# Loading and transposing all four token blocks ahead of the first w1 piece in a dense SiLU layer

## The chip, the cores and the metric

The kernel runs on one core of a Trainium2 chip. The metric is device time in microseconds of one execution. The kernel before was run five times: 128.04, 128.56, 125.96, 125.98 and 127.38 us, with a median of 127.38 us. The first of these executions, 128.04 us, is the one that was profiled; the span of its instructions is 126.7 us.

## The reference

The layer multiplies 2048 tokens of width 640 by a 640 x 1728 matrix, applies SiLU, and multiplies by a 1728 x 640 matrix. Everything is bfloat16.

```python
def reference(x, w1, w2):                      # x [1, 2048, 640], w1 [640, 1728], w2 [1728, 640]
    h = jnp.einsum("bsd,df->bsf", x, w1)
    h = jax.nn.silu(h)
    return jnp.einsum("bsf,fd->bsd", h, w2)
```

## The kernel before, in words

TensorE contracts over the 128 partitions, so the first product needs x transposed, with the width 640 on the partitions. The tile `xT` holds it as five slices of 128 (`DT` = 5) by 2048 tokens. The hidden activations `hT` are produced transposed as well: 13 tiles of 128 hidden columns (`FT` = 13) and a tail of 64 (`FL`). Tokens are worked in four chunks of 512 (`SCH`). One tile of one chunk is five matmuls of 128 x 128 weights against 512 tokens, accumulated in one PSUM bank; ScalarE then applies SiLU into `hT`.

The first chunk is special, because the kernel wants to begin before much has arrived. Its four blocks of 128 tokens, x0 to x3 in this text, are loaded plainly into the tile `x0` (one slice per block) and transposed on TensorE by the helper `turn` (lines 175 to 199). One `turn` waits for its block and for its two PSUM banks, issues five 128 x 128 transposes (line 182), and then has VectorE copy three of the five slices (line 185) and ScalarE copy the other two (line 193) into `xT`. `turn` returns the points in time of these two copies. Blocks 0 and 2 use banks 7 and 6, blocks 1 and 3 use banks 5 and 4, so the turn of block 2 waits for the copies of block 0, and the turn of block 3 for those of block 1. The chunks 1 to 3 come through transposing DMA loads (line 158) straight into `xT`.

The first three hidden tiles (`FA` = 3) of the first chunk are called the opening here. Their columns of w1 are loaded in three pieces along the contraction: piece 0 is slice 0 (96 KB), piece 1 is slices 1 and 2 (192 KB), piece 2 is slices 3 and 4 (192 KB); see `ks` in line 127 and `load_ks` in line 129. The remaining columns of w1 follow in three larger loads (`FG`, line 120).

All these loads are issued from two queues. SP issues, in this order: x0, x1, piece 1, x2, x3, the three larger w1 loads, the fifteen transposing loads, and the w2 loads. ScalarE's queue issues piece 0 and piece 2.[...] The code of each engine is a straight list, executed in order: an engine that waits for a semaphore holds back everything that comes behind it in its own list, the DMA issues included.

TensorE's list in the opening is: nine dummy matmuls on a tile of zeros (line 173), the turns of blocks 0 and 1, and then `k_pass` (lines 216 to 228). A `k_pass(k0, k1, j0, j1)` runs the slices k0 to k1 for the three tiles on the token blocks j0 to j1. The order is: piece 0 on block 0, piece 0 on block 1, piece 1 on blocks 0 and 1, the turn of block 2, piece 2 on blocks 0 and 1, the turn of block 3, then all five slices on block 2, and all five on block 3 (lines 230 to 243). The last pass releases the three SiLU instructions. After the opening, the loop in line 253 runs the other ten tiles of the first chunk, and the loop in line 260 the other chunks. The second product follows the same way and isn't touched.

## Time and profile before

| Quantity | Value |
|---|---|
| Median of five runs | 127.38 us |
| Lowest and highest run | 125.96 and 128.56 us |
| Profiled execution: its own time, its span | 128.04 us, 126.7 us |
| TensorE matmul busy | 122.2 us, 96% of the span |
| TensorE weight loads busy | 58.5 us, 46% |
| ScalarE busy | 40.5 us, 32% |
| VectorE busy | 9.0 us, 7% |
| Transposes of the opening (line 182) | 20, 2.5 us busy |
| Dummy matmuls (line 173) | 9, 2.1 us busy |
| Read from and written to HBM | 5.16 MB and 2.62 MB |

In the views below, PE is TensorE's matmuls, PEld its weight loads, DVE is VectorE, ACT is ScalarE; a q behind an engine's name means its instruction queue, as in SPq for a DMA issued by SP. L208 is line 208 of the kernel before. `ps` is the PSUM tile, `w1s` the tile that holds w1. Times within an execution are microseconds from the start of the span. Matmuls are pipelined and the ends shown are modelled, so the pace of matmuls is read from how many of them fit in a stretch and not from the length of one.

### The profile page before, as it was taken

Reading aid. Unit: us, or ns where it says so; the run is one execution under the profiler, and the core shown is the slowest. Engines: PE = TensorE matmul, PEld = TensorE weight load, DVE = VectorE, ACT = ScalarE, POOL = GpSimd, SP = SyncE. Lnnn points to the kernel's source line nnn. Section 1 sums busy time; section 2 is a strip of 40 time slices with the busy share of each in tenths; the row PEclk is TensorE's granted clock in tenths of the full one; section 3 lists DMA queues with packets and bytes.
Section 4 is the critical chain, followed back from the end, with each engine's and each line's share of the span. In section 5 each row is a group of like instructions: output and inputs, shape, how many; then the busy total and the mean of one; then the engine's idle time right before and its main releaser. Section 6 shows DMA issues by size and latency. Waiting matters only on the chain.

```text
span 126.7 us, 1446 instructions
## 1 busy us (share of the span) xinstructions
PE 122.2 (96%) x625; PEld 58.5 (46%) x636; DVE 9.0 (7%) x16; ACT 40.5 (32%) x70; POOL 0.8 (1%) x7
## 2 busy tenths in 40 slices
PE   8599999999999999999999999999999999999993
PEld 5386444444444444444444444444444443444452
DVE  0120000000000000000000120200004201012021
ACT  5126555555555555555550101010003011010100
POOL 2000000000000000000000000000000000000000
PEclk9999999999999999999999999999999999999999
DMA  5999944448910000000000000000001575111112
GB/s 153 306 376 227 83 97 96 111 94 280 390 49 0 0 0 3 0 0 0 0 5 0 0 0 0 0 0 0 5 0 41 115 265 210 52 52 57 52 54 101
DMA packets 17878, 10.37 MB, mean 82 GB/s; under 512 B 10832, under 2 KB 17872, under 8 KB 17872
## 3 DMA queue, kind: packets, MB, share of 16 engines
q1 hardware_dynamic: 17456, 9.98, 28.9%
q10 hardware_dynamic: 416, 0.30, 0.8%
q8 instruction: 5, 0.08, 0.3%
q14 instruction: 1, 0.01, 0.0%
HBM read 5.16 MB, written 2.62 MB: 61 GB/s over the span
## 4 chain that ended last, share of the span: by engine, by line
PE 93%; DMA 4%; issue 1%; SPq 1%; ACT 0%
PE ps L208 93%; DMA w1s<-in_w_dram 4%; PE ps L182 1%; SPq L89 1%; ACT o_sb L288 0%; SPq L401 0%
## 5 line engine op out<-in xcount | busy, mean ns | idle before, releaser
L208 PE MATMUL ps<-xT,w1s 128*128 128x512 bf16 (+3 forms) x308 | 60.0, 361 | 1.8 <-DMA w1s<-in_w_dram 1.4
L208 PE MATMUL ps<-w2s,hT 128*128 128x512 bf16 (+2 forms) x216 | 45.0, 366 | 0.4 <-issue 0.2
L208 PEld LDWEIGHTS ps<-xT,w1s 128*128 128x128 bf16 (+1 forms) x313 | 28.6, 101 | 32.3 <-DVE xT L185 1.7
L212 ACT ACTIVATE hT<-ps 128x512 bf16<-128x512 f32 x52 | 30.8, 597 | 23.9 <-PE ps L208 23.9
L208 PEld LDWEIGHTS ps<-w2s,hT 128*128 128x128 bf16 x221 | 20.9, 98 | 24.4 <-issue 1.1
L288 ACT CAST o_sb<-ps 128x512 bf16<-128x512 f32 (+1 forms) x8 | 4.4, 546 | 42.2 <-PE ps L208 42.2
L286 DVE CAST o_sb<-ps 128x512 bf16<-128x512 f32 (+1 forms) x9 | 6.1, 677 | 94.2 <-PE ps L208 91.9
L208 PE MATMUL ps<-hT,w2s 128*128 128x512 bf16 x51 | 11.3, 379 | 0.1
L208 PEld LDWEIGHTS ps<-hT,w2s 128*128 128x128 bf16 x52 | 5.1, 98 | 6.1
L288 ACT CAST oT<-ps 128x512 bf16<-128x512 f32 x2 | 1.1, 589 | 11.0 <-PE ps L208 11.0
L193 ACT COPY xT<-ps 128x256 bf16<-128x256 bf16 x4 | 1.5, 372 | 5.2 <-PE ps L182 5.2
L182 PE MATMUL ps<-ident,x 128*128 128x128 bf16 x20 | 2.5, 288 | 0.0
L173 PE MATMUL ps<-z 128*128 128x256 bf16 x9 | 2.1, 418 | 0.4 <-DVE z L124 0.4
L286 DVE CAST oT<-ps 128x512 bf16<-128x512 f32 x2 | 1.3, 687 | 13.7 <-PE ps L208 13.7
L208 PE MATMUL ps<-w2t,hTt 64*128 64x512 bf16 (+2 forms) x17 | 2.2, 366 | 0.0
L182 PEld LDWEIGHTS ps<-ident,x 128*128 128x128 bf16 x20 | 1.9, 130 | 0.6 <-DMA x<-in_x_dram 0.5
L185 DVE COPY xT<-ps 128x384 bf16<-128x384 bf16 x4 | 1.4, 358 | 7.6 <-PE ps L182 7.6
L151 ACT ACT_TABLE_LOAD x1 | 1.3, 1283 | 1.2 <-PEq L401 1.2
L173 PEld LDWEIGHTS ps<-z 128*128 128x128 bf16 x9 | 1.2, 141 | 0.8 <-DVE z L124 0.4
L212 ACT ACTIVATE hTt<-ps 128x512 bf16<-128x512 f32 x2 | 1.2, 597 | 1.1 <-PE ps L208 1.1
L208 PEld LDWEIGHTS ps<-w2t,hTt 64*128 64x128 bf16 x17 | 0.7, 94 | 1.4 <-issue 0.8
L208 PE MATMUL ps<-hTt,w2t 64*128 64x512 bf16 x4 | 0.6, 382 | 0.0
(10 smaller groups left out, 1.5 us busy)
## 6 DMA issues: line engine op xcount, KB each, us to landing
out_dram<-o_sb SPq DMA_DIRECT2D x15, 160.0 KB, 1.9
w2s<-in_w_dram SPq DMA_DIRECT2D x1, 1120.0 KB, 6.5
w2s<-in_w_dram SPq DMA_DIRECT2D x1, 960.0 KB, 8.9
x<-in_x_dram SPq DMA_DIRECT2D x4, 160.0 KB, 3.5
w1s<-in_w_dram SPq DMA_DIRECT2D x1, 640.0 KB, 6.9
w1s<-in_w_dram SPq DMA_DIRECT2D x1, 560.0 KB, 7.8
w1s<-in_w_dram SPq DMA_DIRECT2D x1, 480.0 KB, 5.7
xT<-in_x_dram SPq DMA_TRANSPOSE x15, 2.8
```

What stands on the lines that cost most here:

```text
L89: return tick(eng.dma_start(out=out_ap, in_=in_ap), s, 16)
L151: act.activation(out=warm[:, :], in_=warm[:, :], func=ACT.Silu)
L173: pe.matmul(ps[:, 3, 0:HB], lhsT=z[:, 0:P], rhs=z[:, :], start=True, stop=True)
L182: ins = pe.transpose(dst, x0[:, j, dt * P:(dt + 1) * P], ident[:, :])
L185: r = tick(dve.tensor_copy(out=xT[:, 0:nv, j * P:(j + 1) * P], in_=v[:, 0:nv * P].rearrange("p (k s) -> p k s", s=P),), s_dve)
L193: r = tick(act.copy(out=xT[:, nv:DT, j * P:(j + 1) * P], in_=a[:, 0:(DT - nv) * P].rearrange("p (k s) -> p k s", s=P),), s_act)
L208: return pe.matmul(o, lhsT=l, rhs=r, start=start, stop=stop, skip_group_check=shared)
L212: r = tick(act.activation(out=out_ap, in_=in_ap, func=ACT.Silu), s_act)
L286: r = tick(dve.tensor_copy(out=out_ap, in_=in_ap), s_dve)
L288: r = tick(act.copy(out=out_ap, in_=in_ap), s_act)
```

## The change

It touches two things. The loads of x2 and x3 are issued ahead of all pieces of w1; piece 0 moves from ScalarE's queue to SP's, behind the four blocks of x and ahead of piece 1; piece 2 stays on ScalarE's queue and moves in its list behind the copy of block 0. And all four turns stand ahead of the first w1 matmul in TensorE's list; `k_pass` takes token columns in place of block numbers, piece 0 is run on the tokens 0 to 255 and then on 256 to 511, and pieces 1 and 2 are run on all 512 tokens at once.

```diff
-        ld_k = [load_ks(act, 0), load_ks(sp, 1)]
         for j in (2, 3):
             ld_x[j] = load(sp, x0[:, j, :], x_v[:, j, :])
+        ld_k = [load_ks(sp, 0), load_ks(sp, 1)]
...
         act.activation(out=warm[:, :], in_=warm[:, :], func=ACT.Silu)
-        ld_k.append(load_ks(act, 2))
...
-        t0 = turn(0, 7, 6)
-        t1 = turn(1, 5, 4)
+        turned = turn(0, 7, 6)
+        ld_k.append(load_ks(act, 2))
+        turned += turn(1, 5, 4) + turn(2, 7, 6) + turn(3, 5, 4)
...
-        def k_pass(k0, k1, j0, j1, last=False):
+        def k_pass(k0, k1, t0_, t1_):
             for ft in range(FA):
-                if k0 == 0 and j0 == 0:
-                    wait(pe, bank_free[ft])
                 for k in range(k0, k1):
-                    ins = mm(
-                        ps[:, ft, j0 * P:j1 * P],
-                        w1s[:, k, ft * P:(ft + 1) * P],
-                        xT[:, k, j0 * P:j1 * P],
-                        start=(k == 0 and j0 == 0), stop=(k == DT - 1), shared=True,
-                    )
-                if last:
+                    ins = mm(ps[:, ft, t0_:t1_], w1s[:, k, ft * P:(ft + 1) * P], xT[:, k, t0_:t1_],
+                             start=(k == 0 and t0_ == 0), stop=(k == DT - 1), shared=True)
+                if k1 == DT:
                     silu(hT[:, ft, 0:SCH], ps[:, ft, :], ft, tick(ins, s_pe))
...
-        wait(pe, *t0, ld_k[0])
-        k_pass(0, 1, 0, 1)
-        wait(pe, *t1)
-        k_pass(0, 1, 1, 2)
-        wait(pe, ld_k[1])
-        k_pass(*ks[1], 0, 2)
-        t2 = turn(2, 7, 6)
-        wait(pe, ld_k[2])
-        k_pass(*ks[2], 0, 2)
-        t3 = turn(3, 5, 4)
-        wait(pe, *t2)
-        k_pass(0, DT, 2, 3)
-        wait(pe, *t3)
-        k_pass(0, DT, 3, 4, last=True)
+        wait(pe, *turned[0:4], ld_k[0])
+        k_pass(0, 1, 0, HB)
+        wait(pe, *turned)
+        k_pass(0, 1, HB, SCH)
+        for i, (a, b) in enumerate(ks[1:]):
+            wait(pe, ld_k[i + 1])
+            k_pass(a, b, 0, SCH)
```

The banks that `bank_free[ft]` in the removed wait names had not been used before, so that wait was empty.

## The prediction

> **What bounds the kernel now.** I read the page's chain of waits first, then its groups, then the chain, the timeline and the transfers of the opening alone.

> ```profile
> PE 93%; DMA 4%; issue 1%; SPq 1%; ACT 0%
> ...
> L208 PE MATMUL ps<-xT,w1s 128*128 128x512 bf16 (+3 forms) x308 | 60.0, 361 | 1.8 <-DMA w1s<-in_w_dram 1.4
> ```

> TensorE carries 93% of the chain, and its w1 matmuls idle 1.8 us before them in all. Only the 4% of DMA and the opening's matmuls are open to the change. The chain in order of time gives the opening:

> ```profile
> 1.03 4.86 DMA w1s<-in_w_dram
> 5.90 0.05 issue
> 5.94 1.46 PE ps L208 x6
> 7.41 0.53 PE ps L182 x5
> 7.94 0.77 PE ps L208 x6
> 8.71 0.28 PE ps L182 x5
> 8.98 1.68 PE ps L208 x30
> 10.66 0.05 issue
> 10.71 10.74 PE ps L208 x49
> ```

> Columns: start, length, what. The 30 narrow matmuls ending at 10.66 finish the three opening tiles; from there TensorE runs without a gap worth naming: 10.74/49 = 0.219 us per full matmul. So **the change is worth what it moves the 10.66.** The lines also show the clock. Five transposes take 0.53 us at 7.41 and 0.28 at 8.71; six 256-column matmuls take 1.46 at 5.94, 0.77 at 7.94. The array doubles its pace near 8.1: with 0.213 us slow and 0.109 fast per 256 columns, 0.77 is one slow and five fast. Before that, per the timeline:

> ```profile
> 2.29 1.34 PE L182 MATMUL ps<-ident,x 128*128 128x128 bf16 x10
> ...
> 3.67 0.37 ACT L193 COPY xT<-ps 128x256 bf16<-128x256 bf16 x1 [0.25 <-PE ps L182]
> ...
> 5.07 0.69 PE L208 MATMUL ps<-xT,w1s 128*128 128x128 bf16 x5 [1.43 <-DMA w1s<-in_w_dram]
> ```

> TensorE turns blocks 0 and 1, then stands 1.43 us until piece 0 of w1. The transfers issued from 1 to 5 us, with their time to landing, and the core's state by microsecond (clock share, DMA share and GB/s last):

> ```profile
> x<-in_x_dram SPq DMA_DIRECT2D x2, 160.0 KB, 4.9
> ...
> w1s<-in_w_dram SPq DMA_DIRECT2D x1, 192.0 KB, 4.9
> w1s<-in_w_dram ACTq DMA_DIRECT2D x1, 192.0 KB, 4.8
> w1s<-in_w_dram ACTq DMA_DIRECT2D x1, 96.0 KB, 4.1
> ```
> ```profile
> 1.00:2.00 1.00, 1.00 (x6) 0.75 (x5) 0.00 (x0) 0.78 (x1) 0.35 (x2) 1.00 0.86 210
> 2.00:3.00 1.00, 1.00 (x9) 0.55 (x8) 0.00 (x0) 0.74 (x2) 0.00 (x0) 1.00 0.90 239
> 3.00:4.00 1.00, 0.64 (x6) 0.37 (x5) 0.68 (x2) 0.70 (x2) 0.00 (x0) 1.00 0.84 257
> 4.00:5.00 1.00, 0.00 (x0) 0.00 (x0) 0.03 (x1) 0.05 (x1) 0.00 (x0) 1.00 0.99 335
> ```

> With the issue times of the timeline (x2 1.50, x3 2.01, pieces 0.80, 1.03, 1.29) they land: piece 0 at 4.9, piece 1 at 5.9, piece 2 at 6.1, x2 at 6.4, x3 at 6.8. The DMA engines are full, so order decides, not issue. The clock column shows 1.00 throughout, so it isn't the one that doubles.

> [...]

> **The change part by part.**

> Matmul shape: 48 matmuls become 18, six of 256 columns and twelve of 512; the columns stay 7,680. The 30 narrow ones ran at 1.68/30 = 56 ns, which is 128 columns at the fast rate with weight loads hidden.[...] Full width by itself is worth nothing.

> Order of transfers. SP now issues x2 at about 1.03, x3 at 1.50, piece 0 at 2.0, piece 1 at 2.45, the next w1 groups some 0.45 us later each (one more issue of 0.43 ahead). Landings I estimate from bytes: by the rates above the core has moved 0.21, 0.45, 0.71 and 1.04 MB by 2, 3, 4 and 5 us. In SP's order x2 is complete at 0.49 MB, x3 at 0.655, piece 0 at 0.75, piece 1 at 0.95: moved by 3.2, 3.8, 4.1 and 4.7. Landing follows by 0.4 us (x0: 0.164 MB moved by 1.8, landed 2.2) up to 1.55 (piece 1 now: 0.82 MB with ACT's two by 4.35, landed 5.9). That gives x3 4.2 to 5.35, piece 0 4.5 to 5.7, piece 1 5.1 to 6.3. With sequential x ahead and no second queue beside it I take the lower part: **x3 4.5, piece 0 5.0, piece 1 5.6.**

> Piece 2 is issued behind ACT's wait for block 0's transposes: at 3.1 to 3.5 instead of 1.29. Time to landing 2.2 (x0, nothing beside it) to 4.8 (itself now): 5.3 to 8.3; I take 7.5. Queued behind the waits on ACT are only the copies and this issue; TensorE waits for it.

> TensorE. Block 2 is turned near 3.7 to 4.2, its banks being free (copies end 4.04). Block 3: 4.5 to 5.03; copies, by the rows 0.37, end by 5.5. The piece-0 matmuls start at **5.05**, as now, but without ten transposes among them later (0.53 + 0.28 us). Six of 256 columns at half rate, at the measured 1.46 with dispatch or 1.28 without: done by 6.4. The new wait for all eight copies stands between the two halves, at 5.7, with the whole opening queued behind it; the copies of block 3 end at 5.5, so I cost it at nothing, and at most the 0.65 us by which block 3 may be later. The removed bank wait was empty. Full matmuls cost 0.427 slow (four times 0.106). By 8.1 four of twelve are done; the other eight take 8 × 0.219 = 1.75: end **9.85** instead of 10.66. Piece 2 is needed at 8.5, one microsecond after I expect it; if it comes at 8.3 it still costs nothing. The next w1 group landed at 2.49 + 5.7 = 8.2, now 8.65: hidden behind the opening. The transposing loads start 0.45 later; their fifth landed at 11.81 + 3.6 = 15.4 and is needed 10.8 us after the opening: covered by five microseconds.

> Sum: −0.8, and I keep −0.7 for hand-over between waits. Own time of the profiled execution: 128.04, its span 126.7 and 1.34 around it; that becomes 127.3. It stands 0.66 above the median 127.38, which becomes **126.7**.

> **The rivals.**

> Early clock. The window 1.3 to 4.7 was busy 1.0 us with dummies and 1.34 with transposes, 69%, and didn't release the clock; 4.7 to 8.1, some 82% busy, did. With two more turns, 1.06 us, in it, the first becomes up to 90%, if transposes count. Then pieces 0 and 1 end at 7.0, piece 2 (7.5) is waited for, end 7.5 + 1.31 = 8.8: −1.85, so 125.5.[...]

> Transfers cancel. With landings at their late ends TensorE, which is in order, stands behind block 3 and starts at 6.1: 2.0/0.427 = 4.7 of 15 by 8.1, the rest 2.26, end 10.36: 127.1. At a start of 6.7 nothing is left of the gain. For it: x3 landed at 6.8 before; against: 0.3 MB of w1 was ahead of it then.

> Slower. If the start slips beyond about 6.2, the window 4.7 to 8.1 holds 1.9 us of matmuls and 0.53 of transposes, 71%, like the one that didn't release the clock; release waits until 11.5. From 6.2 that is 5.3/0.427 = 12.4 matmuls slow, 0.57 for the rest, end 12.05: +1.4, so 128.8; from 7.3, 12.65: +2.0, 129.4. Start later than 6.2 is the point that decides.

> The change doesn't do what it says: partly so, since piece 0 stays in halves of 256; no price.

> **How the numbers follow.** Likeliest case 0.46 (126.1 to 127.2); early clock 0.22 (125.0 to 126.0); cancelled 0.18 (126.8 to 127.7); slower 0.14 (128.2 to 129.6). 2%, about what a measurement of this kernel can tell from no change, is 2.55 us: below 124.83 or above 129.93. No case's centre reaches it. The runs shown spread by 2.6 us, so some chance of each: faster 0.05 from the early clock's edge, slower 0.09 from the late clock with a late piece 2; same 0.86. The range 125.4 to 128.9 leaves out the lowest early-clock times (0.07) and the upper half of the slower case (0.08).

> **What would show it.** Right: ten transposes before the first w1 matmul, that matmul at 4.8 to 5.5 released by piece 0, no wait for piece 2, first 512-column tile after the opening near 9.9, the rest of the span as long as now. Wrong: a start after 6.2, 512-column matmuls at 0.427 us beyond 8.1, a wait for piece 2, or TensorE gaps after the opening.

## The result, and the profile after

Over 41 runs the changed kernel has a median of 127.86 us (126.42 to 128.31); the kernel before, over 78 runs, 128.04 us (125.96 to 129.37). The ratio of the medians is 0.9986 (0.9967 to 1.0008, from resampling the runs), that of the means 1.0000 (0.9982 to 1.0018): no change that can be told. A ratio of each kernel's fastest runs alone, those within 1.5% of its own fastest, reads 1.0062 (1.0039 to 1.0084), but that leaves out 43 of the 78 runs of before and none of after, so everything below uses all runs.

The equal medians hide two different shapes. Before falls into two groups: 16 of 78 runs lie under 127.0 us, none between 127.0 and 127.25, and the others reach up to 129.4. After has 3 of 41 under 127.0, and nothing above 128.31. **The change took away the best runs and the worst ones.**

The page of after, chain by engine and the costliest group:

```profile
PE 93%; DMA 3%; SPq 1%; issue 1%; ACT 0%
...
L208 PE MATMUL ps<-xT,w1s 128*128 128x512 bf16 (+2 forms) x278 | 59.9, 384 | 0.6 <-DMA w1s<-in_w_dram 0.4
```

The idle time ahead of the w1 matmuls fell from 1.8 to 0.6 us, and yet the span is 126.8 us where it was 126.7. The chain in order of time (start, length, what):

```profile
1.97 3.72 DMA w1s<-in_w_dram
...
5.73 5.49 PE ps L208 x20
11.22 0.05 issue
11.27 10.74 PE ps L208 x49
```

TensorE begins on w1 at 5.73, when piece 0 lands, 0.66 us later than before. The 20 matmuls are the 18 of the opening and two of the next tile; two full ones are 0.44 us, so the opening ends at 10.78, against 10.66. How fast it ran is seen at its weight loads, one for each matmul of 512 columns (start, length, engine, line, operation, shapes; the last line holds five):

```profile
7.42 0.15 PEld L208 LDWEIGHTS ps<-xT,w1s 128*128 128x128 bf16 x1 [0.27 <-issue]
7.84 0.15 PEld L208 LDWEIGHTS ps<-xT,w1s 128*128 128x128 bf16 x1 [0.28 <-issue]
8.27 0.15 PEld L208 LDWEIGHTS ps<-xT,w1s 128*128 128x128 bf16 x1 [0.28 <-issue]
8.70 0.15 PEld L208 LDWEIGHTS ps<-xT,w1s 128*128 128x128 bf16 x1 [0.27 <-issue]
9.11 0.96 PEld L208 LDWEIGHTS ps<-xT,w1s 128*128 128x128 bf16 x5 [0.27 <-issue]
```

Up to 9.1 us they follow each other by some 0.43 us, which is half rate, and from there by 0.22. So the doubling came at 9.1; before it was at 8.1. And the transfers of after issued from 2.9 to 3.3 us and from 1.4 to 2.1 us (pieces 2 and 0, and among the rest the blocks of x):

```profile
w1s<-in_w_dram ACTq DMA_DIRECT2D x1, 192.0 KB, 4.7
```
```profile
x<-in_x_dram SPq DMA_DIRECT2D x2, 160.0 KB, 2.8
w1s<-in_w_dram SPq DMA_DIRECT2D x1, 96.0 KB, 3.7
```

The blocks come quickly (2.8 us, where x2 took 4.9 before); piece 0 lands at 5.69, piece 2, issued at 3.09, at 7.8.

One relation holds through all profiled executions and says where to look. A kernel's own time less the end of its opening is 128.04 − 10.66 = 117.38 before, 128.25 − 10.78 = 117.47 after, and between 117.38 and 117.48 in the fourteen more taken below. (In e2, e7 and e11 the record of one opening matmul is missing, and the end is counted with it.) Nothing after the opening moves, in any of them. A run of 126.3 us, of which no profile was taken, should by this have had an opening that ended near 8.9.

### The profile page after: what moved, and what is told of

Read it like the earlier page. It is cut to its first block, busy times and chain, and to the rows that moved or that the text cites. A ratio compares the mean times of both kernels' runs of the same rounds, so it can differ in the third digit from the quotient of the medians.

```text
span 126.8 us, 1386 instructions
## 1 busy us (share of the span) xinstructions
PE 123.1 (97%) x595; PEld 57.2 (45%) x606; DVE 9.0 (7%) x16; ACT 40.5 (32%) x70; POOL 0.8 (1%) x7
## 4 chain that ended last, share of the span: by engine, by line
PE 93%; DMA 3%; SPq 1%; issue 1%; ACT 0%
PE ps L208 93%; DMA w1s<-in_w_dram 3%; SPq L89 1%; ACT o_sb L275 0%; SPq L388 0%
## 5 line engine op out<-in xcount | busy, mean ns | idle before, releaser
L208 PE MATMUL ps<-xT,w1s 128*128 128x512 bf16 (+2 forms) x278 | 59.9, 384 | 0.6 <-DMA w1s<-in_w_dram 0.4
L208 PE MATMUL ps<-w2s,hT 128*128 128x512 bf16 (+2 forms) x216 | 45.0, 366 | 0.4 <-issue 0.2
L208 PEld LDWEIGHTS ps<-xT,w1s 128*128 128x128 bf16 (+1 forms) x283 | 27.3, 101 | 33.1 <-issue 1.4
L208 PEld LDWEIGHTS ps<-w2s,hT 128*128 128x128 bf16 x221 | 20.9, 98 | 24.4 <-issue 1.1
L208 PE MATMUL ps<-hT,w2s 128*128 128x512 bf16 x51 | 11.3, 379 | 0.1
L208 PEld LDWEIGHTS ps<-hT,w2s 128*128 128x128 bf16 x52 | 5.1, 98 | 6.1
L208 PE MATMUL ps<-w2t,hTt 64*128 64x512 bf16 (+2 forms) x17 | 2.2, 366 | 0.0
L208 PEld LDWEIGHTS ps<-w2t,hTt 64*128 64x128 bf16 x17 | 0.7, 94 | 1.4 <-issue 0.8
L208 PE MATMUL ps<-hTt,w2t 64*128 64x512 bf16 x4 | 0.6, 381 | 0.0
```

The source lines that it names most:

```text
L208: return pe.matmul(o, lhsT=l, rhs=r, start=start, stop=stop, skip_group_check=shared)
```

## The experiments

My theory after the result: **which run is fast is decided by the moment at which the array's clock doubles**, which is drawn anew in each run, and the change shifts the odds. The rival: only the landings of the transfers and TensorE's start matter. Each kernel ran beside the kernel before; in its several sessions that had medians of 127.70 to 127.99 us, and 54 of 206 runs under 127.0.

| Run | What it is | Runs | Median, us (lowest to highest) | Under 127.0 | Ratio of medians to before |
|---|---|---|---|---|---|
| e1 | before, 6 dummies behind block 1 | 22 | 126.80 (125.76 to 129.19) | 13 | 0.991 (0.990 to 0.998) |
| e9 | before, 3 dummies behind block 0, 4 behind block 1 | 22 | 126.42 (125.97 to 127.11) | 20 | 0.990 (0.988 to 0.998) |
| e3 | before, 1 dummy in place of 9 | 20 | 128.42 (127.38 to 129.33) | 0 | 1.004 (1.001 to 1.007) |
| e4 | after, 1 dummy in place of 9 | 22 | 128.12 (126.96 to 129.50) | 1 | 1.002 (0.999 to 1.004) |
| e2 | after, 6 dummies in the gaps | 14 | 127.40 (126.80 to 128.00) | 3 | 0.996 (0.992 to 1.001) |
| e7 | e2 with piece 2 early | 18 | 126.88 (126.48 to 128.99) | 11 | 0.993 (0.991 to 0.997) |
| e11 | e2 with pieces 0 and 2 early | 22 | 127.25 (126.78 to 129.45) | 5 | 0.997 (0.995 to 1.003) |
| e5 | the new order of loads alone | 6 | 130.62 (128.61 to 131.49) | 0 | 1.022 (1.006 to 1.029) |
| e6 | the new list of TensorE alone | 6 | 129.12 (128.97 to 129.27) | 0 | 1.010 (1.008 to 1.015) |
| e8 | after, opening matmuls 128 wide | 22 | 127.69 (126.13 to 130.00) | 5 | 0.999 (0.996 to 1.004) |
| e10 | after, piece 0 early | 6 | 128.40 (127.98 to 129.37) | 0 | 1.005 (1.002 to 1.014) |
| e12 | after, piece 2 early | 22 | 128.28 (126.67 to 129.09) | 5 | 1.002 (0.995 to 1.006) |
| e13 | before again | 18 | 127.95 (126.19 to 129.12) | 6 | 1.000 (0.991 to 1.002) |
| e14 | after again | 18 | 127.82 (126.29 to 128.64) | 2 | 0.999 (0.996 to 1.001) |

### More and fewer dummies in the kernel before (e1, e9, e3)

```diff
         t0 = turn(0, 7, 6)
+        dummies(3)                  # e9 alone
         t1 = turn(1, 5, 4)
+        dummies(6)                  # e1: 6, e9: 4
```

e3 has `dummies(1)` in place of `dummies(9)`.

> The kernel before with six more dummy matmuls behind the turn of block 1, in the 1.43 us in which TensorE stood. Theory clock phase (the runs of before fall in two groups, 16 of 78 under 127.0 us[...]): with TensorE busy from 0.4 us on, nearly every run falls in the low group, median 126.0 to 126.8, all runs within 1.5 us. Rival transfers (only the landing of the w1 pieces and TensorE's start, 5.07 before and 5.73 after, decide): nothing changes, median 128.0 with the same two groups.

> The kernel before with three dummy matmuls behind the turn of block 0 and four behind that of block 1 (the first filled kernel had six behind block 1 and its profile still stood 1.05 us for block 1, and it had 13 of 22 runs under 127.0 us). Clock phase: the burst from 0.4 to 5 us has no hole, so over 75% of the runs are under 127.0 us, median 126.1 to 126.7. Rival: the rest of the high runs come from late transfers and not from the clock, the share stays near 60% and the median at 126.8.

> The kernel before with one dummy matmul in place of nine. Clock phase: the first burst is cut by 1.7 us, so the low group goes: no run under 127.0, median 128.2 to 128.7. Transfers: 128.0, low group as before.

Dummies compute nothing and touch no transfer, and they decide: the share of runs under 127.0 goes from 0 of 20 with one dummy to 54 of 206 with nine, in the runs beside the experiments, and 20 of 22 with sixteen and no hole. The rival said that e1 changes nothing and that e9 does no better than e1. (In a chain, a step that follows another on TensorE begins at that one's modelled end, about 0.2 us behind its first matmul; real starts are taken from timelines.) In e3's chain the pace stays at half rate to the end of the opening's turns:

```profile
7.11 0.53 PE ps L182 x5
7.65 1.28 PE ps L208 x6
8.93 0.53 PE ps L182 x5
9.46 2.14 PE ps L208 x30
```

The transposes at 8.93 still take 0.53 us, and the end is 11.60. The chain of e9 is one of TensorE alone; a line of its timeline, below it, has the real start of the w1 matmuls:

```profile
4.21 0.85 PE ps L173 x4
5.06 1.46 PE ps L210 x12
6.52 0.28 PE ps L182 x5
6.80 0.65 PE ps L210 x6
7.46 0.28 PE ps L182 x5
7.74 1.68 PE ps L210 x30
```
```profile
4.85 1.67 PE L210 MATMUL ps<-xT,w1s 128*128 128x128 bf16 x12
```

The same order of work and of loads as before, starting at 4.85, against 5.07; both turns take 0.28 us, the end is 9.41, and the 4.86 us of DMA have gone from the chain. e9 has the lowest median of this study, ahead of both kernels compared here. e1 missed part of its runs, probably because block 1 can be late: in its one profile (128.12 us) TensorE stood for it, 1.05 us by the pace of the transposes, which is the hole that e9's three dummies shorten, and the doubling came at 7.8.

### The same kernels once more (e13, e14)

> The kernel before, unchanged, for one more profile. Clock phase: if its time is under 127.0 us, the first w1 matmuls run at full rate (128 columns in 0.056 us from 5 us on) and the opening ends near 9.0; if it is above 127.5, they run at half rate and the opening ends at 10.4 or later. Transfers: the opening's end follows the landing of pieces 1, 2 and block 3, whatever the pace of the matmuls.

> The changed kernel, unchanged, for one more profile. Clock phase: start of the w1 matmuls 5.4 to 6.1 us again, end of the opening between 9.2 (clock early, then held by piece 2) and 11.2 (clock at 10), by the pace of the matmuls. Transfers: the end is again 10.6 to 10.8.

The profile of e13, time 128.38, is a slow draw of the kernel before. Its chain:

```profile
7.14 0.53 PE ps L182 x5
7.67 1.28 PE ps L208 x6
8.95 0.35 PE ps L182 x5
```

The six matmuls that took 0.77 us in the first profile take 1.28, all at half rate; the doubling falls into the transposes at 8.95. With 30 narrow matmuls in 1.68 us from 9.30, the opening ends at 10.98, 0.3 us later, and the time is 0.34 us longer. The transfers don't explain it: piece 1, on which the six matmuls from 5.68 waited, landed at 5.63, against 5.89 in the first profile. The profile of e14 is an early draw of the changed kernel (TensorE, start, length, and what ended the idle time before):

```profile
3.95 0.45 PE L181 MATMUL ps<-ident,x 128*128 128x128 bf16 x5 [0.34 <-DMA x<-in_x_dram]
4.57 0.45 PE L181 MATMUL ps<-ident,x 128*128 128x128 bf16 x5 [0.16 <-DMA x<-in_x_dram]
5.08 2.49 PE L208 MATMUL ps<-xT,w1s 128*128 128x256 bf16 x12
9.17 1.04 PE L208 MATMUL ps<-xT,w1s 128*128 128x512 bf16 x4 [1.60 <-DMA w1s<-in_w_dram]
```

The turns are already fast, the w1 matmuls begin at 5.08, as I had forecast, and pieces 0 and 1 are through by about 7.5. Then TensorE stands 1.60 us for piece 2. Its chain names it: the DMA issued at 3.11 took 6.01 us.

```profile
3.11 6.01 DMA w1s<-in_w_dram
```

Time 128.02: **in this run the early clock was given back, almost all of it, to the wait for piece 2.** Without it the opening would have ended near 9.0. The start, 5.08, is earlier than the 5.4 to 6.1 of the clock theory's expectation, and the end, 10.64, lies in both of them, so it doesn't part them; the pace does.

### Fewer and more dummies in the kernel after, and piece 2 (e4, e2, e7, e12)

```diff
         turned = turn(0, 7, 6)
-        ld_k.append(load_ks(act, 2))       # e7, e12: moved up, behind the first SiLU
-        turned += turn(1, 5, 4) + turn(2, 7, 6) + turn(3, 5, 4)
+        dummies(2)                         # e2, e7; e12 without dummies
+        turned += turn(1, 5, 4)
+        dummies(1)
+        turned += turn(2, 7, 6)
+        dummies(1)
+        turned += turn(3, 5, 4)
+        dummies(2)
```

> The kernel after with one dummy matmul in place of nine. Clock phase: the few low runs (3 of 41) go, the rest stays, since its window is filled by turns and matmuls from 3.4 us on: median 127.8 to 128.2. If transposes don't count as busy, this kernel is as late as the kernel before with one dummy. Transfers: 127.9.

> The kernel after with six more dummy matmuls spread over the gaps between its four turns and the first w1 matmul. Clock phase: TensorE is busy throughout, the clock doubles by about 7 us at the latest, median 126.4 to 127.0, 0.2 to 0.6 us above the filled kernel before, because piece 2 lands at 7.8 us. Transfers: 127.9, as after.

> The filled kernel after (median 127.40) with piece 2 issued on ACT's queue at once, as before the change, in place of behind block 0's copy. Theory late piece 2 (with the clock early, TensorE stood in that kernel until piece 2 landed at 8.92 us): the wait goes, the opening ends near 8.6 instead of 9.6, median 126.5 to 126.9. Rival shared bandwidth (192 KB of piece 2 delay x2, x3 and piece 0 by as much as they save): 127.2 to 127.6, with TensorE's start moved from 5.1 to 5.8 or later.

> The changed kernel with piece 2 issued on ACT's queue at once, nothing filled. Clock phase: most runs have the clock late, and then piece 2 (landed at 7.8) is not waited for, so the bulk stays at 127.3 to 128.3; only the early-clock runs gain: low group larger than 3 of 41, lowest run near 126.0, median 127.4 to 127.8. Rival (piece 2 is what costs in the bulk too): the whole distribution shifts down by 0.4 us or more, median below 127.4.

Filling helps the changed kernel less than half as much as the other: 127.40, above my 127.0. The chain of e2 has the reason, piece 2 again, landed at 8.92:

```profile
3.07 5.85 DMA w1s<-in_w_dram
8.92 0.05 issue
8.97 0.61 PE ps L214 x2
```

With piece 2 issued at once (e7) the median falls to 126.88, as the theory of the late piece said. Its profile (127.08 us) bears out a part of the rival too: the w1 matmuls start at 6.03 where e2 started them at 5.12, because a block of x came late, and the opening ends at 9.70 and not at the forecast 8.6. But the cost of that lies in e12, the same move without dummies: 5 of 22 runs are under 127.0, yet the bulk moved up, to 129.09, which neither theory had. In e12's chain x2 took 3.73 us, and the last two blocks are turned together at 4.80 where after turned them at about 3.9 and 4.7:

```profile
1.03 3.73 DMA x<-in_x_dram
4.75 0.05 issue
4.80 1.25 PE ps L182 x10
6.05 0.64 PE ps L208 x3
```

Here blocks 2 and 3 were late with piece 2 beside them, and the first w1 matmul starts at 5.84 (timeline), only 0.11 us behind that of after. The larger part of the 0.6 us by which this opening ends later (11.40) is the clock: full-width matmuls start 0.427 us apart until near 10.1, one microsecond longer than in after, which is worth half of that. Whether the hole ahead of 4.80 caused the late doubling in most runs of e12, one profile can't show. So the four blocks and piece 2 probably compete for the same 4 us (x2 took 3.73 us here, x2 and x3 a median of 2.8 in after). e4 came out where its clock theory had it, 128.12, with too few low runs in either kernel (1 of 22, 3 of 41) to compare. Whether transposes count for the clock as other matmuls do, it doesn't decide; e8's profile does, below.

### One half of the change alone (e5, e6)

e5 takes the changed kernel's loads and the list of TensorE of before; e6 the reverse.

> The new order of loads with TensorE's list as before. Clock phase: TensorE has only two turns and a hole from about 3.7 to 5.7 us, when piece 0 lands, so the low group shrinks or goes, and the start is 0.65 us later than before: median 128.2 to 128.7. Transfers alone: the same start as the changed kernel, blocks 2 and 3 are there when they are needed, median 127.9.

> TensorE's list of the changed kernel with the loads as before. Both theories: TensorE, in order, stands until block 3 (6.8 us) and begins the w1 matmuls at 7.3, 2.2 us later. Clock phase: the hole from 3.7 to 6.4 keeps the clock at half rate until 8 to 11 us in most runs, median 129.2 to 130.2, widest spread of all. Transfers alone: 2.2 us later with the same clock, less the ten transposes, median 129.4.

Either half alone is slower than both together. e5 is worse than either theory had it: its own profile, with the doubling at about 9.0, ends the opening at 11.23 and gives 128.61; three of its six runs are above 130.9. Its TensorE has only two turns to do until piece 0 lands (1.47 us idle in the profile, start 5.57), so I take the slow runs to be ones in which the doubling came later still; no profile of such a run was taken. e6 waits for blocks 2 and 3 and starts at 6.48, where 7.3 was expected; at 129.12 it lies just under the clock theory's 129.2 to 130.2 and 0.3 us under the rival's 129.4, so the median doesn't part them, and in its six runs the spread is the smallest of all and not the widest. So, as these few runs go, the new list of TensorE is needed to fill the hole which the new order of loads makes, and the new order of loads to feed that list in time.

### Width, and piece 0 (e8, e10, e11)

e8 cuts every opening matmul into pieces of 128 columns. e10 issues piece 0 on ScalarE's queue at 0.8 us; e11 does so in e7.

```diff
-        ld_k = [load_ks(sp, 0), load_ks(sp, 1)]     # behind x2 and x3
+        ld_k = [load_ks(act, 0)]                    # e10, e11: ahead of them
...
+        ld_k.append(load_ks(sp, 1))                 # behind x2 and x3
```

> The changed kernel with each opening matmul cut into 128-column ones, 60 in place of 18, the columns the same. My sum[...]: +0.1 us, median 127.9 to 128.1, the same spread. Rival (full width is worth something, by weight loads or dispatch): at half rate or full rate the opening grows by over 0.5 us, median 128.4 or more.

> The changed kernel with piece 0 back on ACT's queue, issued at 0.8 us. Theory late start (TensorE began at 5.73 and not at the forecast 5.05, because piece 0 waits behind four blocks of x on SP's queue): the start goes to 5.0 to 5.3 and the median falls by 0.2 to 0.3 us, since 0.5 us at half rate are worth half of that: 127.5 to 127.7. Rival (the block of x that is held up by piece 0 now sets the start, or the draw of the clock hides it): 127.8 to 128.1.

> The filled kernel after with pieces 0 and 2 both on ACT's queue at once; only the x-first order on SP and the four turns ahead are left of the change. Clock phase with the pieces in time: median 126.4 to 126.8, like the filled kernel before, so that the order of x in itself brings nothing. Rival (all turns ahead makes TensorE wait for block 3 with full queues): 127.0 or more.

Full width is worth nothing that can be seen (the 0.1 us forecast for e8 was an estimate): 60 matmuls give 127.69, 18 gave 127.86, and the interval of the ratio, 0.996 to 1.004, ends short of the rival's 128.4 (1.005). That the spread grew, to 126.13 to 130.00, I had not expected. e10 shows no gain from an earlier piece 0: in its profile block 3 came late and TensorE stood 1.21 us for it, the rival's mechanism at a higher price than it had (128.40). e11, 127.25, points the same way beside e7's 126.88: with x, piece 0 and piece 2 all early it is x3 that is late, and the chain of its profile goes through a block of x and not through w1. Its expected equality with e1 failed. e10's profile holds more. By microsecond (TensorE's busy time second, its clock share third from the end):

```profile
4.00:5.00 1.00, 0.45 (x5) 0.28 (x5) 0.63 (x2) 0.64 (x2) 0.00 (x0) 1.00 0.84 225
5.00:6.00 1.00, 0.17 (x3) 0.17 (x4) 0.02 (x1) 0.03 (x1) 0.00 (x0) 1.00 0.94 275
6.00:7.00 1.00, 0.68 (x9) 0.41 (x7) 0.36 (x1) 0.37 (x1) 0.00 (x0) 1.00 0.88 268
7.00:8.00 1.00, 1.00 (x5) 0.56 (x5) 0.00 (x0) 0.00 (x0) 0.00 (x0) 0.50 0.98 306
...
9.00:10.00 1.00, 1.00 (x3) 0.15 (x1) 0.00 (x0) 0.00 (x0) 0.00 (x0) 0.50 1.09 376
10.00:11.00 1.00, 0.74 (x4) 0.25 (x4) 0.00 (x0) 0.00 (x0) 0.00 (x0) 0.79 1.87 302
```

Here the view records the clock: the array was fast, fell back to half at 7.0 after three microseconds in which TensorE worked 0.45, 0.17 and 0.68 of the time, and returned 0.42 into the eleventh (0.42 at half and 0.58 at full rate make 0.79). From fall to return are 3.4 us. In the same execution piece 2 took 7.35 us.

The array had doubled its pace at 3.6: there the starts of its transposes go from 0.107 to 0.056 us apart. So the pace changed at 3.6, 7.0 and 10.4, with 3.4 us from each to the next. No other profile has a fall on record (the mean granted clock was 0.987 in e10 and 1.0 in the others), so the 3.4 us are those of e10; the other profiles are laid against the same length. A busy share here is the columns at the pace of the moment and not the modelled lengths. In the 14 profiles that show the moment of the first doubling (in e11 and e14 it falls into a gap), the 3.4 us ahead of it were busy for 75% (e7) to 100%, and the 3.4 us ahead of those for at most 70% (e3), in the first profile 61%, in that of after 60%. The transposes are counted in these shares. In e8 the pace doubles at 5.6:

```profile
2.35 2.52 PE L181 MATMUL ps<-ident,x 128*128 128x128 bf16 x20
4.68 2.76 PE L208 MATMUL ps<-xT,w1s 128*128 128x128 bf16 x36
```

The 3.4 us up to there hold 2.0 us of transposes and 0.8 of other matmuls. In e3 1.9 us of other matmuls and 0.5 of transposes, from 3.5 to 6.9, brought no doubling: the transposes at 8.93 still took 0.53. So transposes count here: without them e8's stretch, which the doubling followed, would hold less than e3's. A cause of the two groups is my estimate from these numbers and is not shown: a stretch of 3.4 us that ends before the hole has grown too large brings the doubling, and one that ends later leaves it to the next or the one after. With e10's 3.4 us laid at every position over the profiled openings, all taken as equally likely, and with the 70 to 75% between the shares above as what a stretch needs, the estimate is that the clock doubles ahead of 6 us in 0.2 to 0.45 of the positions before (two profiles), in 0.4 to 0.7 of those of after (two profiles), and in 0.9 of those of e9 and of e2. The low groups are 54 of 206, 5 of 59, 20 of 22 and 3 of 14: by this estimate an early clock mostly doesn't make a low run in the two kernels that issue piece 2 late. For e3 and e4 the estimate gives none (0 of 20 and 1 of 22). For e1 it gives at most 0.3, by a profile in which block 1 was late, where 13 of 22 runs were low; there it falls short.

## Why the prediction was wrong

The time lies inside the range, 0.18 us under the median of before where I forecast 0.7, and the means are equal: a gain isn't there. The base was off as well: the median of before, 127.38 in five runs, is 128.04 in 78, so 126.7 was 0.66 us too low before any step of the argument.

- **"The clock doubles near 8.1", taken for both kernels: the step that failed.** I read one draw out of one profile and used it as a property of the kernel; I then carried a difference of two such sums over to a median. The five times shown (two at 126.0, three from 127.4) already carried the two groups. In the profiled executions the doubling came at 8.1 and about 9.0 before (e13), at 9.1 and before 4 us after (e14). In the profile after, the 3.4 us from 2.3 to 5.7 were busy for 60% and brought no doubling, and 9.1 for 8.1 costs half of 1.0 us, 0.5.
- **Start at 5.05: mis-sized in the profile.** It was 5.73, because piece 0 landed at 5.69, the very end of my 4.5 to 5.7; I had taken 5.0. At half rate 0.68 us are worth 0.34. Together 9.85 + 0.34 + 0.5 = 10.7, against the 10.78 measured: so the saving of the ten transposes fits as forecast, and the two delays ate it. In e14 the same start was 5.08, so this is a draw too.
- **Piece 2 costed at nothing: the second step that failed, by the size of its landing.** I took 7.5, bound 8.3, and covered it by matmuls at half rate that need it at 8.5. It landed at 7.8, 8.92 (e2) and 9.12 (e14), and with the early clock there is little cover. In that rival I had counted a wait of 0.5 us (7.0 to 7.5); it was 1.60. So the early clock, priced at 125.5, gave 128.02 in e14.
- Two readings of the first profile. The clock column, which I set aside because it reads 1.00 throughout, is that of the array: in e10 it follows the fall to half (0.50 from 7.0 on) and the return at 10.4, and misses only the half rate from the start to 3.6. And the 69% for 1.3 to 4.7 us counted the modelled lengths of transposes; by their pace it is some 61%.
- Matmul shape worth nothing (e8), hidden w1 groups, and transposing loads with room to spare: right. No TensorE gap after the opening was found, and own time less opening is the same to 0.1 us.
- The slower rival: not shown in the changed kernel, whose runs end at 128.64. Its 11.5, which is 8.1 and 3.4 us, was an estimate; changes of pace 3.4 us apart are recorded in e10 alone. A doubling that comes late for want of work is what e3 shows in the kernel before, with transposes still at half rate at 8.93 to 9.46 and the end at 11.60, and probably e5.

What the change does is then this. Its turns keep TensorE busier from 3.4 us on (0.98 of the microsecond from 4 to 5 in the profile after, 0.00 in that of before), which probably is why the late draws of before (129 and more) go; the nine dummies are needed too, since e4, with the same turns and one dummy, has 129.27 and 129.50 among its 22 runs. No transposes are left among the matmuls. But an early clock, which in the kernel before should end the opening near 8.9, runs into piece 2 (1.60 us in e14, 0.72 in e8). The means say that gain and loss are equal; the sizes of the parts were not measured. How much of the lost low group is the wait for piece 2 and how much fewer early draws isn't measured either. The estimate from stretches of 3.4 us speaks for the wait, since it has early draws more often in after than before. e12 has more low runs, 5 of 22 against 5 of 59 for after in both series, but moves x as well.

## What to carry to other kernels

Where times spread in two groups, look for a state that is drawn per run, and forecast the odds of each group and not a shift of the median; a single profile is one draw. Keep TensorE busy without a hole from its first microsecond until the real work flows: seven more dummy matmuls in the kernel before, placed where it would have stood, brought 1% in the median (0.7% in the mean) and a spread of 1.1 us, against 2.5 in the runs beside them. And when a change may let an engine run faster, cost every transfer again at the faster pace.
